# Attention in front of two expert layers: when weights are prepared, when constant rows are filled, and which engine adds the columns of the last batch

## The chip, the cores and the metric

The kernel runs on one core of a Trainium2 chip. The metric is device time in microseconds (us); lower is better. The kernel before was timed at 1121.05 us (median of 3 runs, 1119.55 to 1121.26). The execution that left the profile took 1118.75 us, and the profile's span, from its first to its last instruction, is 1117.0 us.

## The reference, cut to what matters

Three parts are chained. The first is causal attention with a bias made of a running sum of `s`; the second is a sum over 8 experts with a balanced gate; the third is one wide layer with a softplus. The change touches the first part and its seam with the second.

```python
# q, k, v: (2, 8, 576, 64)   s: (2, 8, 576)
cum = np.cumsum(np.maximum(s, 0.0), axis=-1)
bias = -(cum[:, :, :, None] - cum[:, :, None, :])
scores = np.where(causal, -1e9, q @ k.T / 8 + np.minimum(bias, 0.0))
attn = softmax(scores); out = attn @ v
# x = out as (1152, 512): 576 tokens of batch 0, then 576 of batch 1
P = exp(x @ w_gate), rows and columns normalised 8 times in turn
out = sum over e of P[:, e] * (relu(x @ w1[e]) @ w2[e])
out = softplus(out @ w_in) @ w_out
```

## The kernel before, in words

**Attention.** Heads are worked in 8 pairs p = 0 to 7 (pairs 0 to 3 are batch 0, pairs 4 to 7 batch 1), and each pair has 5 units i = 0 to 4: four blocks of 128 query rows, and one block that holds the last 64 rows of both heads. So there are 40 units, numbered n = 0 to 39; unit 6 is (p, i) = (1, 1).

A unit passes through these stages. TensorE computes the scores, adding the running sum by one more product of `bq` and `bk` (L551, L555). VectorE adds the mask and takes the row extreme (L586 to L598). ScalarE takes the exponential (L608), VectorE the reciprocal of its sum (L619), GpSimd multiplies (`eb`, L621). TensorE transposes `eb` (`tr`, L633 to L648), ScalarE copies that to `pt` (L653), and TensorE multiplies by v (`pv`, L665, L675). ScalarE copies the result to `xr` (L724).

The loop at L763 issues, for every n, one step of each stage for a different unit (`LN, LT, LV, LA, LX, LY = 2, 3, 4, 5, 1, 1`), in the order of the letters "YSKAXVWBTED". Every engine runs its instructions strictly in the order issued, so whatever an early instruction waits for holds up all that stand behind it on that engine.

**What is interleaved with it.** Letter K splits the next pair's q and k into a high and a low part (ScalarE L511 `kh`/`qh`, GpSimd L512 `kl`/`ql`). Letter W takes one step of `early_w`, which prepares `w1` of the first expert. Its 32 steps are: two GpSimd sums for each half (L155, L157), splits of ScalarE (L146 `w1h`) and VectorE (L149 `w1l`) with two steps between them, four more GpSimd sums (L162, L164), and six more splits. Letter Y takes up to two steps of `build`, which turns a finished quarter of `xr` into the operands `xh` and `xl` of the expert layer: it forms four differences of column blocks in `xt` (L82), copies high parts on ScalarE (L85) and forms low parts on VectorE (L88). A batch has two builds, c = 0 and c = 1. Only the very last one (batch 1, c = 1, `quick`) has three of its four differences on VectorE; the others have all four on GpSimd, spread over several n.

**Before the loop.** The bias operands `bq`, `bk`, `be` exist twice, set 0 and set 1. Each is cleared and then gets rows of ones or minus ones (`init_bias`, L439): set 1 on VectorE, set 0 on GpSimd. VectorE then takes the running sum (L471, L473), and `cs` holds its two parts (L478, L479). From `cs` come the rows that SP loads into `bk` and `bq` (L452) and `be` (L457). SP issues all loads in program order: after the bias rows of pairs 0 and 1 come q and k of pair 2 (L421), the four raw weight tiles of the first expert (L135, `raw`), v of pair 1 (L428), and the last columns of pair 1's q (L524, `end1h`, `end1l`).

**After it.** The first products of the expert layer (L287) use batch 0 and need ScalarE to copy a partial result (`v`, L295), which stands behind the last build on ScalarE.

Of the kernel before, what the change touches and what calls it, by code (L numbers as in the profile page):

```python
# [20 lines left out]
def attention_moe_ffn(ctx, tc, q, k, v, s, w_gate, w1, w2, w_in, w_out, out):  # L21
    nc = tc.nc
    P = 128
    B, S, H, D = v.shape
# [28 lines left out]
    def f(ap):  # L53
        return ap.bitcast(F32)
# [14 lines left out]
    def build(g, c, xr, xt_pool, quick):  # L69

        h, l = xh[g], xl[g]
        x1, x2 = xr[:, c, :], xr[:, c + 2, :]
        z = x2.rearrange("p (j n) -> p j n", j=2)
        xt = xt_pool.tile([P, 4, HB], F32, tag="xt", name="xt", bufs=1)
        high = [(h[:, B11, c, :], x1[:, :HB]), (h[:, B21:B22 + 1, c, :], z), (h[:, T1:T4 + 1, c, :], xt)]
        low = [l[:, B11, c, :], l[:, B21:B22 + 1, c, :], l[:, T1:T4 + 1, c, :]]
        sums = [(0, x1[:, HB:], x1[:, :HB]), (1, x2[:, HB:], xt[:, 0, :]), (3, x2[:, :HB], xt[:, 1, :]),
                (2, x2[:, HB:], x1[:, HB:])]

        def sum_(n, engine):  # L80
            o, a, b = sums[n]
            engine.tensor_tensor(out=xt[:, o, :], in0=a, in1=b, op=ALU.subtract)  # L82

        def high_(n):
            nc.scalar.activation(out=high[n][0], in_=high[n][1], func=AF.Copy)  # L85

        def low_(n):
            nc.vector.tensor_tensor(out=low[n], in0=high[n][1], in1=f(high[n][0]), op=ALU.subtract)  # L88

        if quick:  # L90
            sum_(3, nc.gpsimd)
            for n in range(3):
                sum_(n, nc.vector)
            for n in range(3):
                high_(n)
            for n in range(3):
                low_(n)
            yield
            return
        high_(0)  # L100
        low_(0)
        yield
        sum_(0, nc.gpsimd)
        yield
        high_(1)
        sum_(3, nc.gpsimd)
        sum_(1, nc.gpsimd)
        yield
        low_(1)
        sum_(2, nc.gpsimd)  # L110
        for _ in range(3):
            yield
        high_(2)
        yield
        low_(2)
        yield
# [281 lines left out]
    with tc.manual_schedule():  # L398
# [3 lines left out]
        with ExitStack() as att:  # L402
# [36 lines left out]
            def init_bias(x, engine):  # L439
                for t in (bq_t[x], bk_t[x], be_t[x]):  # L440
                    engine.memset(f(t), 0.0)
                for j in range(2):
                    for t, cols, one in ((bq_t[x], slice(0, S), 1.0), (bk_t[x], slice(0, S), -1.0),
                                         (be_t[x], slice(j * REM, (j + 1) * REM), 1.0)):
                        engine.memset(f(t[j * D:j * D + 4, cols]), one)

            def load_bias(p):
                for j in range(2):
                    h = 2 * p + j
                    x = c8d[h] if p > 1 else f(cs[h:h + 1])  # L450
                    for t, r, cols in ((bk_t, 2, slice(0, S)), (bq_t, 0, slice(0, S))):
                        (nc.sync if p > 0 or j == 0 else nc.scalar).dma_start(  # L452
                            out=f(t[p % BB][j * D + r:j * D + r + 2, :]), in_=x)
                for j in range(2):
                    h = 2 * p + j
                    x = c8d[h, :, NB * P:] if p > 1 else f(cs[h:h + 1, :, NB * P:])
                    nc.sync.dma_start(out=f(be_t[p % BB][j * D:j * D + 2, j * REM:(j + 1) * REM]), in_=x)  # L457
# [10 lines left out]
            c8 = eb_tile(B * H, "c8")  # L468
            nc.vector.memset(ones, 1.0)
            init_bias(1, nc.vector)  # L470
            nc.vector.tensor_scalar(s_sb, s_sb, 0.0, 8.0, ALU.max, ALU.mult)  # L471
            for a, b, first in ((0, 2 * P, 0.0), (2 * P, S, c8[:, 2 * P - 1:2 * P])):
                nc.vector.tensor_tensor_scan(c8[:, a:b], one_row[:, a:b], s_sb[:, a:b], first, ALU.mult, ALU.add)  # L473
            init_bias(0, nc.gpsimd)
            cs = ac.tile([B * H, 2, S], F32R, name="cs")
            c8d = dr.tile([B * H, 2, S], F32, name="c8d")
            for a, b in ((0, 2 * P), (2 * P, S)):
                nc.scalar.activation(out=cs[:, 0, a:b], in_=c8[:, a:b], func=AF.Copy)  # L478
                nc.vector.tensor_tensor(out=cs[:, 1, a:b], in0=c8[:, a:b], in1=f(cs[:, 0, a:b]), op=ALU.subtract)  # L479
            load_bias(0)  # L480
            make_identity(nc, ident)

            W = NB * P
# [238 lines left out]
            def do_X(n):  # L722
                for pv, o, p in xs.get(n - LX, ()):
                    nc.scalar.activation(out=o, in_=pv, func=AF.Copy)  # L724
                    if p is not None and p % NP >= NP // 2:
                        g, c = p // NP, p % NP - NP // 2
                        building.append(build(g, c, xr, ap2, g + 1 == B and c == 1))
# [28 lines left out]
                        split_ends(p + 1)  # L756

            def do_W(n):
                if n >= 3:
                    next(prework, None)  # L760

            do = dict(S=do_S, T=do_T, V=do_V, A=do_A, X=do_X, Y=do_Y, B=do_B, E=do_E, K=do_K, D=do_D, W=do_W)
            for n in range(nu + LA + LX + 1):  # L763
                now[0] = n
# [228 lines left out]
        x = -1  # L993
# [92 lines left out]
```

## Time and profile before

| what | value |
|---|---|
| median of 3 runs | 1121.05 us |
| profiled execution | 1118.75 us |
| span of its profile | 1117.0 us |
| TensorE (PE) busy | 1080.4 us, 97% |
| VectorE (DVE) busy | 737.8 us, 66% |
| ScalarE (ACT) busy | 528.1 us, 47% |
| GpSimd (POOL) busy | 419.6 us, 38% |

A busy share here is an average over the whole span. The attention takes about the first 121 us, and the expert products follow almost without a gap. Times in rows are counted from the span's start. A row of the timeline is start, duration, engine, line, operation, output and inputs, shape, count, and in brackets the idle time of the engine before it with what ended that idle time. SPq is the queue of the engine that issues loads.

### The profile page before, as it was taken

Reading aid. Unit: us, or ns where it says so; the run is one execution under the profiler, and the core shown is the slowest. Engines: PE = TensorE matmul, PEld = TensorE weight load, DVE = VectorE, ACT = ScalarE, POOL = GpSimd, SP = SyncE. Lnnn points to the kernel's source line nnn. Section 1 sums busy time; section 2 is a strip of 40 time slices with the busy share of each in tenths; the row PEclk is TensorE's granted clock in tenths of the full one; section 3 lists DMA queues with packets and bytes.
Section 4 is the critical chain, followed back from the end, with each engine's and each line's share of the span. In section 5 each row is a group of like instructions: output and inputs, shape, how many; then the busy total and the mean of one; then the engine's idle time right before and its main releaser. Section 6 shows DMA issues by size and latency. Waiting matters only on the chain.

```text
span 1117.0 us, 18144 instructions
## 1 busy us (share of the span) xinstructions
PE 1080.4 (97%) x6692; PEld 951.8 (85%) x6692; DVE 737.8 (66%) x1641; ACT 528.1 (47%) x1246; POOL 419.6 (38%) x493
## 2 busy tenths in 40 slices
PE   4989999999999999999999999999999999999998
PEld 3767789898988988889888898889889898888887
DVE  4456645847878778787878888775555575465553
ACT  3988644233443434334343443334334267656551
POOL 5876411134423324142341523413020065555552
PEclk9999999999999999999999999999999999999999
DMA  5222102032122322223132222311112111111001
GB/s 171 85 78 66 40 1 76 3 112 94 67 94 95 125 83 87 95 94 121 60 114 95 95 90 75 129 58 38 38 39 76 38 39 38 39 38 38 1 11 75
DMA packets 30424, 78.48 MB, mean 70 GB/s; under 512 B 6048, under 2 KB 10656, under 8 KB 30336
## 3 DMA queue, kind: packets, MB, share of 16 engines
q1 hardware_dynamic: 27768, 68.93, 19.1%
q0 software_dynamic: 2560, 8.39, 1.9%
q8 instruction: 52, 0.85, 0.3%
q14 instruction: 36, 0.29, 0.1%
q10 hardware_dynamic: 8, 0.01, 0.0%
HBM read 66.00 MB, written 10.82 MB: 69 GB/s over the span
## 4 chain that ended last, share of the span: by engine, by line
PE 82%; DVE 7%; ACT 5%; POOL 3%; issue 2%; SPq 1%; DMA 0%; POOLq 0%; DVEq 0%; ACTq 0%
PE py L376 41%; PE ph L287 31%; PE ph L351 4%; POOL a L259 2%; PE sc L551 1%; POOL a L258 1%; PE pv L665 1%; DVE a L256 1%; DVE hl L265 1%; PE tr L639 1%; ACT hh L262 1%; ACT a L251 1%; ACT eb L608 1%; PE tr L633 1%; ACT a L250 1%
## 5 line engine op out<-in xcount | busy, mean ns | idle before, releaser
L376 PE MATMUL py<-w2h,hh 128*128 128x512 f32 x720 | 287.2, 399 | 7.4 <-DVE acc L388 6.1
L376 PE MATMUL py<-w2h,hl 128*128 128x512 f32 x720 | 285.2, 396 | 1.0 <-DVE hl L238 1.0
L376 PE MATMUL py<-w2l,hh 128*128 128x512 f32 x720 | 285.2, 396 | 0.0
L287 PE MATMUL ph<-xh,w1h 128*128 128x288 f32 x896 | 265.1, 296 | 2.5 <-ACT v L295 2.5
L287 PE MATMUL ph<-xh,w1l 128*128 128x288 f32 x896 | 264.8, 296 | 0.0
L287 PE MATMUL ph<-xl,w1h 128*128 128x288 f32 x896 | 263.3, 294 | 0.0
L287 PEld LDWEIGHTS ph<-xh,w1h 128*128 128x128 f32 x896 | 167.9, 187 | 20.0 <-ACT v L295 2.8
L287 PEld LDWEIGHTS ph<-xl,w1h 128*128 128x128 f32 x896 | 168.3, 188 | 16.5
L287 PEld LDWEIGHTS ph<-xh,w1l 128*128 128x128 f32 x896 | 168.2, 188 | 0.0
L376 PEld LDWEIGHTS py<-w2h,hl 128*128 128x128 f32 x720 | 135.7, 188 | 34.1 <-DVE hl L238 1.6
L201 POOL TENSOR_TENSOR w2l<-raw,w2h 128x512 fp32r<-128x512 f32 x40 | 55.4, 1384 | 287.4 <-ACT w2h L199 287.4
L235 ACT ACTIVATE hh<-ph 128x288 fp32r<-128x288 f32 x192 | 78.8, 412 | 159.8 <-DVE ph L337 81.2
L376 PEld LDWEIGHTS py<-w2h,hh 128*128 128x128 f32 x720 | 135.5, 188 | 21.2 <-DVE acc L388 6.8
L376 PEld LDWEIGHTS py<-w2l,hh 128*128 128x128 f32 x720 | 135.9, 189 | 11.6
L295 ACT ACTIVATE v<-ph 128x288 f32<-128x288 f32 x128 | 51.0, 411 | 171.7 <-PE ph L287 164.8
L391 DVE SCALAR_TENSOR_TENSOR acc<-py,gate,acc 128x512 f32<-128x512 f32 x126 | 94.0, 746 | 54.2 <-PE py L376 54.0
L894 POOL TENSOR_TENSOR cm<-cm,ct 128x512 f32<-128x512 f32 x32 | 45.1, 1409 | 202.5 <-DVE ct L892 202.5
L238 DVE SCALAR_TENSOR_TENSOR hl<-ph,hh 128x288 fp32r<-128x288 f32 x192 | 86.7, 454 | 30.5 <-ACT hh L235 28.7
L149 DVE TENSOR_TENSOR w1l<-raw,w1h 128x512 fp32r<-128x512 f32 (+1 forms) x144 | 99.8, 694 | 8.3 <-ACT w1h L146 8.2
L265 DVE TENSOR_TENSOR hl<-a,hh 128x288 fp32r<-128x288 f32 x64 | 38.0, 594 | 71.9 <-ACT hh L262 71.9
L146 ACT ACTIVATE w1h<-raw 128x512 fp32r<-128x512 f32 (+1 forms) x144 | 82.9, 577 | 1.6 <-PE ph L287 1.6
L258 POOL TENSOR_TENSOR a<-a,a 128x288 f32<-128x288 f32 x64 | 51.8, 809 | 78.8 <-DVE a L256 61.4
(182 smaller groups left out, 1766.1 us busy)
## 6 DMA issues: line engine op xcount, KB each, us to landing
raw<-in_w SPq DMA_DIRECT2D x64, 512.0 KB
f<-in_w_in SPq DMA_DIRECT2D x16, 512.0 KB
f<-in_w_out SPq DMA_DIRECT2D x16, 512.0 KB
wd<-cm POOLq DMA_DIRECT2D x32, 256.0 KB, 3.2
raw<-wd SPq DMA_DIRECT2D x16, 512.0 KB
out<-acc SPq DMA_DIRECT2D x9, 256.0 KB
vv<-in_v SPq DMA_DIRECT2D x8, 256.0 KB
qk<-in_k SPq DMA_DIRECT2D x7, 288.0 KB
```

Of the source, the lines that this page charges most:

```text
L146: nc.scalar.activation(out=hi[:, o], in_=t[:, src], func=AF.Copy)
L149: nc.vector.tensor_tensor(out=lo[:, o], in0=t[:, src], in1=f(hi[:, o]), op=ALU.subtract)
L201: (nc.gpsimd if i else nc.vector).tensor_tensor(out=lo, in0=t[:, r], in1=f(hi), op=ALU.subtract)
L235: nc.scalar.activation(out=hh, in_=z, func=AF.Relu)
L238: nc.vector.scalar_tensor_tensor(out=hl, in0=z, scalar=0.0, in1=f(hh), op0=ALU.max, op1=ALU.subtract)
L258: nc.gpsimd.tensor_tensor(out=a2, in0=a1, in1=a2, op=ALU.subtract)
L265: nc.vector.tensor_tensor(out=hl, in0=a3, in1=f(hh), op=ALU.subtract)
L287: nc.tensor.matmul(o, u, v, start=(start and c == 0 and n == 0), stop=(c == 1 and n == 2), skip_group_check=True)
L295: nc.scalar.activation(out=t, in_=self.a, func=AF.Copy)
L376: nc.tensor.matmul(py[t], u, v, start=(k == 0 and n == 0), stop=(k == NF - 1 and n == 2))
L391: nc.vector.scalar_tensor_tensor(out=a, in0=py, scalar=gate_t[0][:, t, e:e + 1], in1=a, op0=ALU.mult, op1=ALU.add)
L894: nc.gpsimd.tensor_tensor(out=m, in0=m, in1=f(t), op=ALU.add)
```

## The change

Three edits.

1. `init_bias` is cut in two. It now only clears; a new `init_ones` fills the rows of ones. For set 0 both follow each other on GpSimd as before. For set 1 the clearing stays ahead of the running sum on VectorE, and its six fills move behind the running sum and the first loads of bias rows.
2. `do_W` starts at n = 9 where it started at n = 3, so each step of the first expert's weights comes six units later. The 32 steps fit still: the last comes at n = 41.
3. `build` takes the path with three differences on VectorE for both builds of the last batch. For c = 0 it yields between the parts, so that they spread over n = 41 to 43.

```diff
@@ build
-        if quick:
+        if g + 1 == B:
+
             sum_(3, nc.gpsimd)
             for n in range(3):
                 sum_(n, nc.vector)
             for n in range(3):
                 high_(n)
+                if not quick:
+                    yield
             for n in range(3):
                 low_(n)
+                if not quick:
+                    yield
             yield
             return
@@ init_bias
             def init_bias(x, engine):
                 for t in (bq_t[x], bk_t[x], be_t[x]):
                     engine.memset(f(t), 0.0)
+
+            def init_ones(x, engine):
                 for j in range(2):
                     for t, cols, one in ((bq_t[x], slice(0, S), 1.0), (bk_t[x], slice(0, S), -1.0),
                                          (be_t[x], slice(j * REM, (j + 1) * REM), 1.0)):
@@ before the loop
             init_bias(0, nc.gpsimd)
+            init_ones(0, nc.gpsimd)
...
             load_bias(0)
+            init_ones(1, nc.vector)
             make_identity(nc, ident)
@@ the loop
             def do_W(n):
-                if n >= 3:
+                if n >= 9:
                     next(prework, None)
```

Lines of the changed kernel are 5 to 9 higher than the same lines before.

VectorE in the opening, before: the last three fills of set 1 (`bq_92`, `bk_94`, `be_96`) stand ahead of the running sum `c_112` and its parts `cs`.

```order
L445 MEMSET bq_92 4x576
L445 MEMSET bk_94 4x576
L445 MEMSET be_96 4x64
L471 TENSOR_SCALAR s_sb<-s_sb 16x576
L473 SCALAR_TENSOR_TENSOR c_112<-one_row,s_sb 16x256
L473 SCALAR_TENSOR_TENSOR c_112<-one_row,c_112,s_sb 16x320
L479 TENSOR_TENSOR cs<-c_112,cs 16x256
L479 TENSOR_TENSOR cs<-c_112,cs 16x320
```

VectorE in the opening, now: the running sum follows the last clearing directly.

```order
L446 MEMSET be_96 128x128
L478 TENSOR_SCALAR s_sb<-s_sb 16x576
L480 SCALAR_TENSOR_TENSOR c_112<-one_row,s_sb 16x256
L480 SCALAR_TENSOR_TENSOR c_112<-one_row,c_112,s_sb 16x320
L487 TENSOR_TENSOR cs<-c_112,cs 16x256
L487 TENSOR_TENSOR cs<-c_112,cs 16x320
L452 MEMSET bq_92 4x576
L452 MEMSET bk_94 4x576
L452 MEMSET be_96 4x64
```

All six fills moved from ahead of `s_sb` to behind `cs`.

GpSimd in the first units, before: the sums of the raw weights (`raw_187`, `raw_189`) stand between the scalings of `eb`, whose `st_201` to `st_204` are those of units 0 to 3.

```order
L512 TENSOR_TENSOR ql<-qk,qh 128x576
L621 TENSOR_SCALAR eb<-eb,st_201 128x128 x2
L155 TENSOR_TENSOR raw_187<-raw_187 128x256
L621 TENSOR_SCALAR eb<-eb,st_202 128x256 x2
L157 TENSOR_TENSOR raw_187<-raw_187 128x256
L621 TENSOR_SCALAR eb<-eb,st_203 128x384 x2
L155 TENSOR_TENSOR raw_189<-raw_189 128x256
L621 TENSOR_SCALAR eb<-eb,st_204 128x512 x2
```

GpSimd in the first units, now: nothing of the weights until unit 7.

```order
L521 TENSOR_TENSOR ql<-qk,qh 128x576
L630 TENSOR_SCALAR eb<-eb,st_201 128x128 x2
L630 TENSOR_SCALAR eb<-eb,st_202 128x256 x2
L630 TENSOR_SCALAR eb<-eb,st_203 128x384 x2
L630 TENSOR_SCALAR eb<-eb,st_204 128x512 x2
L521 TENSOR_TENSOR kl<-qk,kh 128x576
L630 TENSOR_SCALAR eb<-eb,st_205 128x576
L521 TENSOR_TENSOR ql<-qk,qh 128x576
L630 TENSOR_SCALAR eb<-eb,st_206 128x128 x2
L630 TENSOR_SCALAR eb<-eb,st_201 128x256 x2
L160 TENSOR_TENSOR raw_187<-raw_187 128x256
```

The first sum of `raw_187` moved from behind unit 0's scaling to behind unit 6's.

VectorE at the end of the attention, before: the two builds of batch 1 (`xl_77`), of which only the second has differences (`xt`) here; `st_204` is unit 39's.

```order
L88 TENSOR_TENSOR xl_77<-xr,xh_75 128x288
L617 TENSOR_REDUCE st_204<-st_204 128x1
L619 RECIPROCAL st_204<-st_204 128x1
L88 TENSOR_TENSOR xl_77<-xr,xh_75 128x2x288
L88 TENSOR_TENSOR xl_77<-xt,xh_75 128x4x288
L82 TENSOR_TENSOR xt<-xr 128x288
L82 TENSOR_TENSOR xt<-xr,xt 128x288 x2
```

VectorE at the end of the attention, now.

```order
L82 TENSOR_TENSOR xt<-xr 128x288
L82 TENSOR_TENSOR xt<-xr,xt 128x288 x2
L626 TENSOR_REDUCE st_204<-st_204 128x1
L628 RECIPROCAL st_204<-st_204 128x1
L88 TENSOR_TENSOR xl_77<-xr,xh_75 128x288
L88 TENSOR_TENSOR xl_77<-xr,xh_75 128x2x288
L88 TENSOR_TENSOR xl_77<-xt,xh_75 128x4x288
```

Three differences of the first build came onto VectorE ahead of unit 39's reciprocal, and its low parts went behind it; the second build is as it was.

## Rows read from the trace of the kernel before

**Rows 1.** Windows, one pair each (three in the second): length, busy PE PEld DVE ACT POOL, clock.

```profile
47.69:59.07 11.38, 11.38 (x124) 8.85 (x125) 6.09 (x34) 10.87 (x32) 9.94 (x15) 1.00 0.30 87
59.07:101.27 42.20, 37.44 (x370) 28.05 (x371) 25.21 (x106) 36.36 (x101) 31.90 (x42) 0.96 0.24 69
101.27:112.66 11.39, 11.39 (x124) 8.85 (x125) 5.84 (x33) 9.69 (x30) 4.75 (x9) 1.00 0.25 80
```

**Rows 2.** Timeline of the opening, 0 to 12 us.

```profile
0.75 0.40 SPq L460 DMA_DIRECT2D s_sb<-in_s  x1
...
1.66 0.43 SPq L421 DMA_DIRECT2D eb<-in_q  x1
...
3.02 0.54 DVE L445 MEMSET bq<- 4x576 f32 x1
...
5.17 0.80 PE L551 MATMUL sc<-eb 64*128 64x128 f32 x4 [5.17 <-DMA eb<-in_q]
...
5.65 0.45 DVE L471 TENSOR_SCALAR s_sb<-s_sb 16x576 f32<-16x576 f32 x1
...
8.34 0.48 DVE L479 TENSOR_TENSOR cs<-c,cs 16x320 fp32r<-16x320 f32 x1 [0.22 <-ACT cs L478]
...
9.69 0.58 SPq L452 DMA_DIRECT2D bq<-cs  x1
...
11.54 0.80 PE L551 MATMUL sc<-bk,bq 64*128 64x128 f32 x2 [5.57 <-DMA bq<-cs]
```

**Rows 3.** Timeline of units 3 and 4, 23 to 25 us.

```profile
23.01 0.72 POOL L155 TENSOR_TENSOR raw<-raw 128x256 f32<-128x256 f32 x1 [5.32 <-DMA raw<-in_w]
23.29 2.04 SPq L524 DMA_DIRECT2D end1l<-ql  x2
...
24.25 1.15 PE L633 MATMUL tr<-ident,eb 128*128 128x128 f32 x4 [5.48 <-POOL eb L621]
```

**Rows 4.** Windows of 1 us: length, PE busy, granted clock, DMA share, GB/s.

```profile
23.00:24.00 1.00, 0.00 (x0) 0.50 0.99 352
...
77.00:78.00 1.00, 1.00 (x11) 0.64 0.09 20
```

**Rows 5.** Chain of waits that ended last: start, length, what.

```profile
18.01 4.93 DMA raw<-in_w
...
34.21 1.06 PE sc L555 x8
...
36.30 0.37 PE tr L633 x2
...
49.42 0.59 PE tr L633 x4
```

**Rows 6.** DMA issues of the page: count and KB of each.

```profile
raw<-in_w SPq DMA_DIRECT2D x64, 512.0 KB
...
qk<-in_k SPq DMA_DIRECT2D x7, 288.0 KB
```

**Rows 7.** Timeline of units 20 to 24, 61 to 76 us.

```profile
61.98 0.62 ACT L146 ACTIVATE w1h<-raw 128x512 fp32r<-128x512 f32 x1
...
64.35 1.41 POOL L512 TENSOR_TENSOR kl<-qk,kh 128x576 fp32r<-128x576 f32 x1 [1.58 <-ACT kh L511]
...
67.80 1.28 DVE L149 TENSOR_TENSOR w1l<-raw,w1h 128x512 fp32r<-128x512 f32 x1
...
69.67 0.42 PE L555 MATMUL sc<-kh,end0h 128*128 128x320 f32 x1 [1.15 <-DVE st L586]
...
71.11 1.63 POOL L621 TENSOR_SCALAR eb<-eb,st 128x128 f32<-128x128 f32 x4
...
75.27 0.63 PE L633 MATMUL tr<-ident,eb 128*128 128x128 f32 x4 [1.52 <-ACT pt L653]
```

**Rows 8.** Line L82 on VectorE from 60 to 126 us: duration least/median/most in ns.

```profile
L82 DVE TENSOR_TENSOR xt<-xr,xt x2: 457/668/878, 123.6 to 124.6; 128x288 f32<-128x288 f32 x2
```

**Rows 9.** Timeline of the first expert products, 126 us.

```profile
126.62 0.40 PE L287 MATMUL ph<-xh,w1h 128*128 128x288 f32 x1 [2.52 <-ACT v L295]
```

## The prediction, made blind

> **What bounds the kernel now.** I read the busy shares first: TensorE is busy 97% of the span, so a change to the attention can only pay where TensorE stands still there, or runs slowly. Windows cut at the first transposes of a pair show where that is. A pair without trouble takes 11.38 us with TensorE busy throughout, and so does the last full one, 11.39 [rows 1]. Three pairs in a row, 4 to 6 less their edges, take 42.20 us in place of 3 x 11.38 = 34.14: 8.1 us are lost there. The timeline of the opening shows TensorE waiting 5.57 us for the first bias row `bq` [rows 2]. The timeline of the units behind it shows one long stop: TensorE waits 5.48 us for GpSimd's scaling of unit 1, and GpSimd itself sat 5.32 us in front of it, at the first sum of the raw weights, for their load [rows 3]. The clock by windows is 0.50 (the 1.2 GHz level) when TensorE comes back [rows 4]. The chain of waits agrees on the place: it runs through that load for 4.93 us [rows 5]. Last, TensorE waits 2.52 us on the seam to the expert layer, for a copy `v` on ScalarE [rows 9]. Behind that point the expert products run almost without a gap, and the change leaves them as they are. So I expect what is saved before the seam to stay saved.
>
> **Term 1, the fills.** Before, VectorE starts the first fill at 3.02 and the running sum at 5.65 [rows 2]. Six fills go from there, 2.63 us. The sum, `cs`, the bias loads and every load that SP issues behind them start earlier by that much, if `s_sb` has arrived at 3.02. The trace shows no wait for it, since VectorE came late. It is issued at 0.75. The short load `bq` was issued at 9.69 and used at 11.54, 1.85 us later; the 288 KB load `eb<-in_q` was issued at 1.66 and used at 5.17, 3.51 us later [rows 2, 6]. So `s_sb` arrives between 2.60 and 4.26, and the term is 2.63 down to 2.63 - (4.26 - 3.02) = 1.39. It is 36 KB, far nearer to the short load; I take 2.6.
>
> The Trainium skill, "DMA: Bandwidth & Descriptors", section "Anatomy of one DMA — SWDGE (gpsimd) path", puts the fixed part of one transfer at about 2.0 us. An estimate by it has `s_sb` there at about 2.8, no wait; the 1.85 us of the trace agrees.
>
> The fills cost the same 2.63 us where they go. VectorE's part of `cs` ends at 8.82, now 6.19, so they end at 8.82 again. What covers them is the bias row's load: its product starts at 11.54 - 2.63 = 8.91 and takes 0.80 [rows 2], and VectorE's first masking waits for that. If the cover failed the price would be what sticks out, under 0.3 us. SP's loads into set 1 come behind pair 0's loads and must wait for the fills too: those before them on SP run past 8.82.
>
> **Term 2, the stop.** With the sums gone from units 3 to 6, GpSimd goes from unit 0's scaling straight to unit 1's. That was held 5.32 us; TensorE had finished its earlier work at 24.25 - 5.48 = 18.77 and had nothing else. I take 5.48, with 5.32 below [rows 3]. The sums come at unit 9, by then about 27 us, when the tiles loaded from 18.01 on have long landed; nobody waits for them before the splits of unit 13, and the first product with these weights comes after the attention.
>
> **Term 3, the clock.** From unit 1's transposes to the next pair's first, TensorE took 36.30 - 24.25 = 12.05 us; over the same work a pair of windows later it took 59.07 - 49.42 = 9.65 [rows 1, 3, 5]. The difference of 2.40 is the stretch at the 0.50 clock, which began while TensorE stood still [rows 4]. Without the stop I count it as saved; the other end is 0, if the clock falls all the same.
>
> **Term 4, what is late next.** The last columns `end1l` are issued up to 25.33 and used at unit 9's scores at 34.21 [rows 3, 5]. Terms 1 to 3 together bring these scores to 34.21 - 10.5 = 23.7, but the loads only to 25.33 - 2.63 = 22.70. With the short load's time behind its issue, 11.54 - 10.27 = 1.27, they arrive at 23.97: a wait of 0.3. The load of `eb<-in_q` needed 5.17 - 2.09 = 3.08 behind its issue: 25.78, a wait of 2.1. And the way is busy: two tiles of 288 KB and four of 512 KB are ahead, 2.69 MB, at 352 GB/s 7.6 us [rows 4, 6]. Counted from 18.01 - 2.63 = 15.4 that is 23.0, with 1.27 more 24.3, a wait of 0.6. I take -0.6, bounds 0 and -2.1. Opening: 2.6 + 5.5 + 2.4 - 0.6 = 9.9 us.
>
> **Term 5, the lossy pairs.** The splits move by six units, and three things change among units 19 to 24. (a) ScalarE's `w1h` of 0.62 leaves unit 20, where ScalarE is full. (b) VectorE's `w1l` of 1.28 leaves unit 22, where TensorE waits 1.15 us for the masking right behind it. (c) GpSimd gets the four second sums in units 19 to 22, where `build` has its differences. Two of them, 2 x 0.72 [rows 3], come between `kl` at 64.35 and the scalings at 71.11 [rows 7], a stretch in which GpSimd never rests. So GpSimd reaches those scalings at 71.11 - 0.62 (an earlier `kh`) + 1.44 = 71.9, while TensorE would be ready for them 0.62 + 1.15 earlier than before: it waits for GpSimd in place of VectorE and gains next to nothing at this point. But ScalarE and VectorE then run ahead, and the next wait, 1.52 us for a copy to `pt` behind the large `xh` [rows 7], shrinks. I take +1.2 of that 1.52. If with fewer gaps the clock does not fall at 77 [rows 4], more than 1 us is added. Bounds: +4.0 (half of the 8.1 us) and -1.5 (the sums, all in TensorE's way).
>
> The splits that come to units 35 to 38 add at most 2 x 0.62 us to ScalarE's 9.69 in a pair of 11.39 [rows 1, 7]: 10.93, hidden. Without that cover, -1.2.
>
> **Term 6, the seam.** Before, the four differences of build c = 0 run on GpSimd behind unit 39's scaling; the large `xh`, the evacuation of the last `xr` and the last build queue up behind them on ScalarE, and at its end the copy `v`. With three on VectorE, the large `xh` has its input some us earlier, and the last build starts when TensorE delivers. VectorE pays by its own row, 0.46 each, 0.88 where GpSimd's difference runs beside it [rows 8]: 3 x 0.46 = 1.4 to 1.8 us, ahead of unit 39's reciprocal, in a place where it took a low part of `build` before. The gain ends where TensorE's wait does, 2.52 [rows 9]. Since the large `xh` also goes ahead of unit 38's copies to `pt`, I take half a us off: +2.0, bounds 0 (ScalarE as late as before) and 2.5.
>
> Against this edit speaks the Trainium skill, "SBUF — State Buffer", section "Who interferes with whom": a VectorE instruction with two inputs in SBUF contends with a GpSimd instruction that reads SBUF. By it one of the three differences runs at the slow figure, as 878 against 457 ns shows [rows 8]. Term 6 would be 2.0 with it and about 2.4 without.
>
> **Sum.** 9.9 + 1.2 + 2.0 = 13.1 us. The profiled execution of 1118.75 us becomes 1105.7, its span of 1117.0 becomes 1103.9. That execution lies 2.3 us under the median of the runs; I subtract from the median: 1121.05 - 13.1 = 1108.0.
>
> **Rivals.**
> - *The opening gives less.* `s_sb` is late (-1.2), `end1l` is late (a further -1.5), and the clock falls in the opening anyway (-2.4). For it: the transfers are near saturation at 352 GB/s, and nothing in the trace shows when `s_sb` lands. Against it: the opening's gap gets shorter, not longer. 13.1 - 5.1 = 8.0: 1113.0 us.
> - *The lossy pairs come free too.* Term 5 at its upper end: 13.1 + 2.8 = 15.9, 1105.2 us. For it: the fall of the clock there follows two waits of which one goes. Against it: the second build, units 26 to 31, has its splits as before.
> - *The change doesn't do what it says.* GpSimd's wait for the raw load goes, but TensorE then waits in the same place for another load of the saturated stretch, and the seam stays. Only the fills' 2.6 us and about as much lost again in term 5: 1121 us.
> - *Slower: the weights become the bound.* Their last split ends six units later, and the next expert's two raw tiles, whose buffers it frees, load later by six units, about 14 us (6 x 11.38 / 5). If that expert's preparation waited for them, ScalarE and VectorE would queue behind it and TensorE with them. It decides from the point where the tiles come over 13.1 us after they are wanted; with 5 us more, 1126. Against it: a tile takes 4.93 us [rows 5] and is wanted only in the first expert's products, behind 126.62.
>
> **Chances.** The forecast, 1106 to 1111 us by itself, 0.60; the weak opening 0.22; free pairs 0.12; no effect 0.03; slower 0.03. The range from 1103.5 to 1113.5 takes in the first three with most of their bounds. A measurement of this kernel tells about 0.2%, 2.2 us, from no change. Faster by more than that 0.94, same 0.03, slower 0.03.
>
> **What would show it.** In the profile after: the running sum at about 3.0 and the first `bq` product at 8.9 (term 1); no wait of GpSimd for `raw` and no TensorE stop over 1 us before 25 us (term 2); clock 1.00 through 20 to 30 us (term 3); unit 9's scores with a wait under 1 us for `end1l` (term 4); the three pairs in about 41 us, with GpSimd as what TensorE waits for near unit 23 (term 5); TensorE's wait for `v` under 1 us (term 6). A new stop of several us ahead of the `end` columns, or a seam still waiting 2.5 us, would make the prediction wrong.

## The result, and the profile after

The changed kernel takes 1107.55 us (median of 4 runs, 1107.13 to 1108.51) against 1120.86 us before (1119.55 to 1121.26, 4 runs): a ratio of 0.9884, 95% interval 0.9867 to 0.9902, or 11.0 to 14.9 us. The forecast was 1108.0. The profiled execution took 1107.13 us with a span of 1105.4.

One profile of each kernel is one execution, so both kernels were profiled twice more (e9 to e12 below). The table puts the three profiled executions of each side by side: starts in the timeline, in us (the windows of [rows 1] are cut 0.07 later).

| point | before | after | change of the means |
|---|---|---|---|
| first transposes of unit 1 | 24.25, 25.56, 25.97 | 17.38, 17.08, 16.23 | -8.4 |
| first transposes of pair 1 | 36.23, 37.59, 37.65 | 29.80, 29.83, 30.63 | -7.1 |
| first transposes of pair 3 | 59.00, 60.36, 60.43 | 52.58, 53.55, 53.40 | -6.8 |
| first transposes of pair 6 | 101.20, 102.56, 102.59 | 93.60, 96.01, 96.83 | -6.6 |
| first gate product `pg`, behind the seam | 131.82, 133.16, 133.18 | 122.25, 124.65, 125.48 | -8.6 |
| end of the span | 1117.0, 1118.2, 1118.2 | 1105.4, 1107.9, 1110.2 | -10.0 |

So the attention gives 8.6 us, and the 13.3 between the medians hold more than the terms of the prediction name. The three pairs differ: up to `pg` the first one gives 9.6 us and the other two 8.1 on the mean, up to the end of the span 11.6 and about 9. These are rows of the timeline of after, first profile.

```profile
2.88 0.43 DVE L478 TENSOR_SCALAR s_sb<-s_sb 16x576 f32<-16x576 f32 x1
...
8.65 0.44 PE L560 MATMUL sc<-bk,bq 64*128 64x128 f32 x1 [2.87 <-DMA bq<-cs]
...
11.57 1.09 PE L560 MATMUL sc<-bk,bq 64*128 64x384 f32 x1
...
13.38 1.41 PE L560 MATMUL sc<-bk,bq 64*128 64x512 f32 x1
...
16.58 0.38 PE L642 MATMUL tr<-ident,eb 128*128 128x128 f32 x2
...
17.38 0.66 PE L642 MATMUL tr<-ident,eb 128*128 128x128 f32 x4
...
20.00 1.29 SPq L533 DMA_DIRECT2D end1h<-qh  x2
...
27.49 0.38 PE L564 MATMUL sc<-kh,end1h 128*128 128x320 f32 x1 [2.14 <-DMA end1h<-qh]
...
65.60 0.68 PE L642 MATMUL tr<-ident,eb 128*128 128x128 f32 x2 [1.56 <-POOL eb L630]
...
106.27 0.57 DVE L82 TENSOR_TENSOR xt<-xr 128x288 f32<-128x288 f32 x1
107.29 1.32 DVE L82 TENSOR_TENSOR xt<-xr,xt 128x288 f32<-128x288 f32 x2 [0.45 <-ACT xr L733]
...
116.61 0.39 ACT L300 ACTIVATE v<-ph 128x288 f32<-128x288 f32 x1
...
117.06 0.40 PE L292 MATMUL ph<-xh,w1h 128*128 128x288 f32 x1
```

The running sum starts at 2.88 and the first `bq` product at 8.65, where [rows 2] has 5.65 and 11.54. The 5.48 us stop of [rows 3] is gone: unit 1's transposes follow unit 0's within 0.8 us. A new stop stands at 27.49, 2.14 us for `end1h`. Near unit 20 TensorE now waits for GpSimd, where [rows 7] has VectorE and ScalarE. At the seam `v` is ready when it is wanted; the 2.52 us of [rows 9] are gone. The chain of waits of the same kernel (start, length, what) shows what the new stop hangs on:

```profile
20.65 6.70 DMA end1h<-qh
```

And the windows (length; busy PE PEld DVE ACT POOL; clock, DMA share, GB/s) show a pair without trouble, the lossy three one by one, and their sum:

```profile
29.87:41.27 11.40, 11.40 (x125) 8.86 (x125) 5.59 (x33) 10.35 (x30) 9.70 (x15) 1.00 0.29 88
...
52.65:65.60 12.95, 11.39 (x123) 8.77 (x124) 5.88 (x29) 12.20 (x35) 11.89 (x16) 1.00 0.26 77
65.60:80.01 14.41, 13.16 (x124) 10.00 (x124) 10.16 (x36) 11.91 (x33) 12.36 (x16) 0.88 0.24 69
80.01:93.67 13.66, 12.37 (x124) 9.15 (x125) 8.79 (x40) 12.02 (x34) 9.71 (x15) 1.00 0.11 29
52.65:93.67 41.02, 36.92 (x370) 27.92 (x371) 24.84 (x105) 36.13 (x100) 33.96 (x45) 0.96 0.20 58
```

The three pairs take 41.02 where [rows 1] has 42.20. In the middle one the clock mean of 0.88 shows a fall that came behind the stop of 1.56.

### The profile page after: what moved, and what is told of

The parts are those of the page before. It is cut to its first block, busy times and chain, and to the rows that moved or that the text cites. A ratio compares the mean times of both kernels' runs of the same rounds, so it can differ in the third digit from the quotient of the medians.

```text
span 1105.4 us, 18149 instructions
## 1 busy us (share of the span) xinstructions
PE 1077.6 (97%) x6692; PEld 949.1 (86%) x6692; DVE 739.5 (67%) x1644; ACT 526.1 (48%) x1246; POOL 417.8 (38%) x490
## 4 chain that ended last, share of the span: by engine, by line
PE 82%; DVE 6%; ACT 4%; POOL 4%; issue 2%; DMA 1%; POOLq 0%; SPq 0%; ACTq 0%; DVEq 0%
PE py L381 41%; PE ph L292 32%; PE ph L356 4%; POOL a L264 2%; PE sc L560 2%; DVE hl L270 1%; PE pv L674 1%; POOL a L263 1%; DVE a L261 1%; PE tr L648 1%; ACT hh L267 1%; ACT eb L617 1%; DMA end1h<-qh 1%; PE sc L564 1%; ACT a L256 1%
## 5 line engine op out<-in xcount | busy, mean ns | idle before, releaser
L381 PEld LDWEIGHTS py<-w2l,hh 128*128 128x128 f32 x720 | 135.5, 188 | 11.6
```

The lines of the kernel that those rows point to most:

```text
L381: nc.tensor.matmul(py[t], u, v, start=(k == 0 and n == 0), stop=(k == NF - 1 and n == 2))
```

## The experiments

Differences of times are against the 1120.56 us (16 runs) or 1120.73 us (8 runs) that the kernel before took on the same chip.

**e1: the weights' steps alone, on the kernel before.**

```diff
-                if n >= 3:
+                if n >= 9:
```

> The kernel before with the weights' steps from unit 9 alone. Theory A (the opening is set by when the end columns land, and that time hangs on SP's queue, which this edit alone does not move): TensorE no longer waits for GpSimd, but waits about 3.6 us for end1h at unit 9's scores, which start at about 30.0 in place of 34.2; with 1.2 us from the lossy pairs the kernel gains about 5.3 us, 1115.6. Rival B (the terms add up as in the prediction): the stop, the clock and the lossy pairs give 5.5 + 2.4 - 0.6 + 1.2 = 8.5 us, 1112.4, with a wait under 1 us for end1h.

Measured 1115.46 us (ratio 0.996, 0.9946 to 0.9973): 5.1 less, the amount that theory A says. Its timeline:

```profile
29.42 0.38 PE L555 MATMUL sc<-kh,end1h 128*128 128x320 f32 x1 [1.06 <-DMA end1h<-qh]
...
121.29 0.61 PE L287 MATMUL ph<-xh,w1h 128*128 128x288 f32 x1 [2.48 <-ACT v L295]
```

The wait for `end1h` takes the place of the stop, though it is 1.06 and not the 3.6 expected; the seam still waits. So this edit alone brings the raw load's stop down to a wait for the next load in line.

**e2: the fills alone, on the kernel before.**

```diff
+            def init_ones(x, engine):
...
+            init_ones(0, nc.gpsimd)
...
+            init_ones(1, nc.vector)
```

> The kernel before with the six fills behind the running sum alone. Theory A: every load comes 2.6 us earlier, so the raw weights land earlier and GpSimd's wait for them ends earlier by as much: 2.6 us gained, 1118.3, with unit 1's transposes at 21.6 in place of 24.25. Rival B (what counts is when TensorE gets through pair 0, which in the changed kernel came only 1.3 us earlier, since its products there run at half the speed of later ones): 1.3 us, 1119.6.

Measured 1116.97 us (0.9969, 0.9959 to 0.9979): 3.6 less, a microsecond more than the 2.6 of theory A. Its timeline:

```profile
21.24 0.89 PE L637 MATMUL tr<-ident,eb 128*128 128x128 f32 x4 [3.88 <-POOL eb L625]
```

The stop for the raw weights is 3.88 where the kernel before has 5.48, 5.75 and 6.27. In that one profile the load is used 4.73 us behind its issue (15.28 to 20.01); in the three executions of the kernel before that takes 5.00, 6.32 and 6.59. With such a spread in one kernel it is not shown that the earlier issue made the load faster, and where the extra microsecond comes from stays open.

**e3: the column sums of the last batch alone, on the kernel before.**

```diff
-        if quick:
+        if g + 1 == B:
```

> The kernel before with batch 1's first build on VectorE alone. Theory A: the seam gives its 2.0 us by itself, 1118.9, TensorE's wait for v falls from 2.5 us to under 0.6, and the first expert product starts about 0.6 us later. Rival B: the last build is late whatever the first does, no gain, 1120.9.

Measured 1116.9 us (0.997, 0.996 to 0.9981): 3.7 less. In its profile the wait for `v` is gone, and from pair 6's transposes to `pg` it takes 132.00 - 103.61 = 28.39 us; before takes 30.62, 30.60 and 30.59. The seam gives 2.2, then, as A says. The other 1.5 us of the timed difference are not at the seam; its one profile does not show where they are.

**e4: the two raw tiles of `w2` loaded later, on the kernel after.** They stand ahead of `end1h` on SP and are wanted only in the expert layer. Here they go to unit 9.

```diff
-            for which in (1, 2):
-                for i in range(2):
-                    load(0, which, i)
+            for i in range(2):
+                load(0, 1, i)
...
+                if n == 9:
+                    for i in range(2):
+                        load(0, 2, i)
```

> The changed kernel with the two raw w2 tiles of the first expert loaded behind unit 9's step in place of before the loop; all else as it is. Theory A: the 1 MB that goes from ahead of the end columns brings end1h about 3 us earlier, TensorE's wait of 2.14 us for it goes, and the kernel gains 2.1 us: 1105.4. Rival B (end1h is late because SP issues it late, not because of what is ahead in the queues): the wait stays at 2.1 us, 1107.5. Rival C: the two tiles now hold up bias rows or v of a later pair on SP, and a new wait eats the gain: 1107.5 or more.

Measured 1107.02 us (0.9892, 0.9876 to 0.9907), no different from after. No wait for `end1h`: pair 1 starts at 26.37, 3.4 earlier than after. But the tiles now stand ahead of the next bias rows. Its timeline and its chain:

```profile
39.20 0.67 PE L560 MATMUL sc<-bk,bq 64*128 64x128 f32 x2 [0.57 <-DMA bq<-c8d]
```

```profile
35.23 3.83 DMA bq<-c8d
```

The next pair takes 12.57 us instead of 11.4, and a part of the gain is given back there. Two things qualify the 3.4. Unit 1's transposes come at 16.25 against 17.38, so 1.1 of it is there before `end1h` matters: here the products of 512 columns in pair 0 ran at full speed, which varies between executions (e10). And SP itself comes to `end1h` earlier:

```profile
16.25 0.43 SPq L433 DMA_DIRECT2D vv<-in_v  x1
16.72 0.56 SPq L434 DMA_DIRECT2D vv<-in_v  x1
17.39 1.78 SPq L533 DMA_DIRECT2D end1h<-qh  x2
```

In after the row of `end1h` stands at 20.00. SP issues two tiles fewer, and the two loads of v behind the tiles take 0.43 and 0.56 us to issue where they took 1.12 and 1.55. So the wait comes of the two tiles, but rival B is not ruled out as a part of it: how much they cost at SP's issue and how much in the queues is not separated.

**e5: the same two tiles at unit 34**, behind the last bias rows.

```diff
+                if n == 34:
+                    for i in range(2):
+                        load(0, 2, i)
```

> The changed kernel with the two raw w2 tiles loaded behind unit 34, where the loads of attention are through. In e4 (behind unit 9) the wait for end1h went, pair 1's first transposes came at 26.44 in place of 29.87, but the next pair waited for a bias row behind the two tiles and 1.2 us went again. Theory A (both waits are the price of what is ahead in the queues): neither wait is left, all of the 3.4 us of pair 1 reach the first expert product, at 110.3 in place of 113.6, and the kernel gains 3.4 us on the changed one: 1104.1. Rival B (the wait for the bias row comes of SP's order, not of the tiles): as in e4, 2.1 us, 1105.4.

Measured 1105.72 us (0.9866, 0.985 to 0.9882). Neither wait is left, and the clock stays at 1.00 up to pair 4. Pair 3's first transposes come at 49.12, 3.5 to 4.4 us ahead of the three executions of after; the first expert product comes at 110.23, as A had it (110.3). The median fell by 1.8 only, near the number of B, though the wait that B names is not there. The profile shows the rest behind the seam: here the clock falls behind the second long stop of the wide layer (1020 to 1023 us), which it does not in the first profile of after. A row of pair 0, for e6, and for the lossy pairs a row of its timeline and its window:

```profile
11.58 1.09 PE L560 MATMUL sc<-bk,bq 64*128 64x384 f32 x1
...
62.17 0.68 PE L641 MATMUL tr<-ident,eb 128*128 128x128 f32 x2 [1.58 <-POOL eb L629]
```

```profile
49.12:90.20 41.08, 38.25 (x371) 29.10 (x369) 24.83 (x104) 36.30 (x101) 34.03 (x45) 0.92 0.20 58
```

**e6: e5, and TensorE kept busy before the first bias row.** 17 products of ones by ones, whose results nobody reads, around the first scores.

```diff
+            def warm_up(k):
+                for _ in range(k):
+                    nc.tensor.matmul(warm[:, :P], ones, ones, start=True, stop=True)
+
+            warm_up(9)
```

> e5 with 9 products of ones by ones on TensorE ahead of the first scores and 8 between them and the first bias product, where TensorE only waits; their result is not used. Theory A (pair 0's products take twice as long as later ones because TensorE was idle before them and its clock is at the lower level, though the clock column reads 1.00 there): the 512-column bias products of pair 0 fall from about 0.8 to 1.4 us to about 0.4, unit 0's transposes come at 15.0 to 15.5 in place of 16.58, and 1.1 to 1.6 us are gained on e5: 1102.8. Rival B (they are long because of operands in float32 and of waits for masking): durations as before, no gain, 1104.1. Rival C: the products stand in the way and the first bias product is later than 8.65.

Measured 1106.02 us (0.9868, 0.9854 to 0.9882): nothing over e5. Its timeline:

```profile
10.63 0.63 PE L560 MATMUL sc<-bk,bq 64*128 64x384 f32 x1
...
14.84 0.68 PE L650 MATMUL tr<-ident,eb 128*128 128x128 f32 x2 [0.74 <-POOL eb L638]
...
24.04 0.38 PE L566 MATMUL sc<-kh,end1h 128*128 128x320 f32 x1 [0.46 <-DMA end1h<-qh]
```

The bias product of 384 columns takes 0.63 us, where e5 and after have 1.09: A's durations hold, pair 0's products run at full speed from 8.7 us on. (The products of 512 columns tell nothing here: e5 too has 0.80 for them.) What they win is taken by GpSimd's scaling (0.74) and `end1h` (0.46): pair 1 starts at 26.38, in e5 at 26.35.

**e7: after without the four second sums of the first expert.**

```diff
-            if x < NX:
+            if 0 < x < NX:
...
+            if x == 0:
+                for _ in range(4):
+                    yield
```

> The changed kernel without the four second sums of the first expert's raw weights on GpSimd (units 19 to 22); the output of that expert is then not the reference's. Theory A (term 5: GpSimd has become what TensorE waits for near unit 23): the wait of 1.56 us at unit 20's transposes goes or falls under 0.4, and the three pairs from 52.65 take 0.5 to 1.2 us less than 41.02. Rival B (the next wait, for the copy to pt and for masking, takes it): the wait goes but the three pairs take 41.0 as before.

One execution, 1112.32 us, with 4.36 us of waiting for `end1h` in its opening, so only the lossy pairs are read. Timeline and window:

```profile
68.14 0.68 PE L645 MATMUL tr<-ident,eb 128*128 128x128 f32 x2 [0.27 <-POOL eb L633]
71.19 0.63 PE L645 MATMUL tr<-ident,eb 128*128 128x128 f32 x4 [1.02 <-ACT pt L665]
```

```profile
56.42:98.61 42.19, 37.49 (x371) 28.15 (x370) 24.55 (x104) 36.83 (x102) 32.01 (x42) 0.96 0.19 57
```

GpSimd's wait of 1.56 shrinks to 0.27: the second sums did make it. But ScalarE's copy is late next, by 1.02, and the three pairs take 42.19, inside the 41.02 to 43.43 of after. In this one execution taking the sums away gains nothing, as B has it.

**e8: e5, with one step of `build` for each unit instead of two, up to unit 39.**

```diff
-                for _ in range(2):
+                for _ in range(1 if n < 40 else 2):
```

> e5 with one step of build per unit in place of two before unit 40, so that batch 0's two builds spread over units 21 to 36. Theory A (the three lossy pairs lose about 7 us because the pieces of a build come together and stand ahead of masking and of the copies to pt): the loss falls by 2 to 4 us, to about 1101. Rival B (the loss is the sum of the work on ScalarE and VectorE, wherever it stands, or mostly the one large piece of xh and xl): no gain, 1104.1, or a loss where the second build now meets the splits of units 32 to 35.

Measured 1104.06 us (1103.63 to 1104.57; 0.985, 0.9837 to 0.9864), the fastest of all. Timeline and window:

```profile
64.42 0.89 PE L641 MATMUL tr<-ident,eb 128*128 128x128 f32 x4 [0.81 <-POOL eb L629]
```

```profile
50.16:88.24 38.08, 35.60 (x371) 26.85 (x369) 24.56 (x105) 34.93 (x100) 32.94 (x42) 1.00 0.21 63
```

The wait of 1.58 becomes 0.81, the clock stays at 1.00, and the three pairs lose 38.08 - 34.14 = 3.9 us in place of 6.9. Most of these 3.0 us are not waits: TensorE stands still for 38.08 - 35.60 = 2.5 us here and for 41.08 - 38.25 = 2.8 in e5, while its busy time is 2.65 us less, because in e5 the clock falls (0.92) and here it does not. That the shorter wait kept it up is likely and not shown, since falls vary between executions of one kernel (below). The opening of this profile was a microsecond later than that of e5; `pg` comes 1.7 us earlier, and the medians, of 5 and 4 runs, are 1.7 apart too.

**e9 and e10: the kernel after as it is, twice more. e11 and e12: the kernel before, twice more.** Another chip, one execution each.

> The changed kernel as it is, looked at once more. In the profiles so far the wide layer at the end shows one of two pictures behind the same stop of about 2.0 us (TensorE waits for VectorE's acc): the granted clock falls to 0.50 for some 3 to 4 us (before, and the single edits e1, e2, e3, and e5, e8), or it stays 1.00 (after, e4, e6, e7). From the product behind the copy v (pg) to the end that is about 985.0 us with the fall and 983.2 without. Theory A: whether it falls varies between executions of one kernel and is no effect of the change; then about half of the looks at after show it, and the time from pg to the end is 985 in those. Theory B: the kernel decides it (its place in time at the start shifts everything behind); then this look shows none again, 983.2 us, and both looks at before show it.

> The same kernel, a third look. A: a fall in one of the two looks, or in both; B: none in either, clock 1.00 from 1015 to 1040 us, 983.2 us from pg to the end. In either case the first products of pair 0 run at their half-speed durations again (1.41 us for 512 columns), and the wait for end1h is between 1 and 4 us, by how fast the raw tiles land.

> The kernel before as it is, looked at once more. A: the clock stays at 1.00 behind the wide layer's stop in one of the two looks at before, and pg to the end is then about 983.2 us. B: it falls in both, 985 us. The stop for the raw load near 24 us is between 4.9 and 6.2 us (5.48 in the first look, 6.10 in e3, whose opening is that of before).

> The same, a third look at before: A no fall in one of the two, B a fall in both. The differences of the two kernels over the attention alone (first product of the opening to pg) should be 9.6 us in any of these looks, give or take the 1 us by which the raw load's landing varies.

Measured 1109.78 and 1111.95 us for after, 1119.97 and 1119.94 for before. The wide layer has three long stops. Behind the second, which the expectations mean, there is a fall in e10 and none in e9, a fall in e11 and none in e12. Theory A holds: one kernel does both. (The 1.41 us that e10's text expects again for 512 columns were 0.80; its 384 columns still took the half-speed 1.09.) The windows of e10, then those of e12, and one of the first profile of after, behind its third stop:

```profile
26.00:28.00 2.00, 1.14 (x4) 1.18 (x5) 0.00 (x0) 0.33 (x2) 0.00 (x0) 0.70 0.55 164
28.00:30.00 2.00, 2.00 (x15) 1.78 (x16) 0.74 (x4) 0.00 (x0) 0.03 (x1) 0.50 0.04 12
...
53.40:96.83 43.43, 40.98 (x371) 31.22 (x370) 24.72 (x104) 36.87 (x102) 33.96 (x45) 0.84 0.18 55
...
1025.00:1030.00 5.00, 3.69 (x13) 3.21 (x13) 4.43 (x10) 3.23 (x9) 3.07 (x4) 0.69 0.01 3
```

```profile
982.00:988.00 6.00, 6.00 (x28) 5.41 (x27) 3.81 (x8) 2.83 (x7) 3.25 (x4) 0.72 0.00 1
...
1035.00:1040.00 5.00, 4.11 (x24) 3.72 (x25) 4.22 (x8) 3.04 (x7) 3.49 (x4) 1.00 0.01 3
```

```profile
1076.00:1082.00 6.00, 6.00 (x27) 5.44 (x28) 2.59 (x7) 2.19 (x5) 3.18 (x5) 0.72 0.23 87
```

The wide layer stops TensorE three times for VectorE's `acc`, by some 5.6 to 6.1 us in all, in every execution. Behind the third stop the clock falls in all six. Behind the first two there is one fall in each execution of before (in e12 behind the first), and none, none and one after. From `pg` to the end that makes 985.2, 985.0 and 985.0 us before, and 983.2, 983.3 and 984.7 after. The two of after with and without show that such a fall costs about 1.5 us. Another 0.3 is the first stop itself, 1.94 to 1.97 us before and 1.63 to 1.66 after; what shortened it stays open.

Not expected: in e9 and e10 the clock falls in the opening as well. The timelines of e9 and e10, in that order:

```profile
26.96 0.38 PE L564 MATMUL sc<-kh,end1h 128*128 128x320 f32 x1 [1.91 <-DMA end1h<-qh]
```

```profile
26.86 0.61 PE L564 MATMUL sc<-kh,end1h 128*128 128x320 f32 x1 [2.67 <-DMA end1h<-qh]
```

and the windows of e9:

```profile
28.00:30.00 2.00, 2.00 (x20) 1.53 (x20) 1.33 (x7) 0.07 (x1) 0.81 (x2) 0.67 0.03 7
30.00:32.00 2.00, 2.00 (x22) 1.55 (x24) 0.51 (x6) 1.67 (x4) 1.03 (x2) 0.50 0.03 8
...
53.55:96.01 42.46, 37.56 (x372) 28.00 (x370) 24.77 (x104) 36.79 (x102) 34.03 (x45) 0.96 0.19 56
```

A stop of 2.14 us was followed by full speed, one of 1.91 by the 1.2 GHz level. So the length of a stop alone does not tell whether the clock falls. The rise at the start varies as well: the first products of 512 columns took 1.41 us in the first profile of after and in e9, 0.80 in e10. Of this rise the Trainium skill says in "TensorE: Matmul & The Clock Gate", section "What's actually happening", that its point depends on where the first product falls in a window which runs freely; these executions agree. For the falls no run shows more than that they vary.

## Why the prediction was right, and where it was not

The sign and the parts of the kernel were right, and so was the time, in part by luck, as the end of this section shows. By its own terms, with two rows of the timeline of after, first profile, and one of its windows, for term 4:

```profile
17.18 1.12 SPq L433 DMA_DIRECT2D vv<-in_v  x1
18.34 1.55 SPq L434 DMA_DIRECT2D vv<-in_v  x1
```

```profile
15.00:27.00 12.00, 10.22 (x85) 7.31 (x85) 6.95 (x37) 10.64 (x31) 9.67 (x16) 1.00 0.87 281
```

- **Term 1, the fills: right.** Forecast 2.6. `s_sb` is not waited for, the first `bq` product comes 2.9 us earlier each time, and unit 0's transposes 2.5 us on the mean (17.90, 18.95, 18.84 to 16.58, 16.29, 15.43). In the first pair it is only 1.3, since there the late products of pair 0 ran slower after (1.41 us for 512 columns) than before (0.89). The fills' new place cost nothing that shows. The 2.0 us that the prediction takes from the Trainium skill, "DMA: Bandwidth & Descriptors", section "Anatomy of one DMA — SWDGE (gpsimd) path", stand there for loads issued by GpSimd. `s_sb` is issued by SP; that it had landed is shown by the row at 2.88, which has no wait.
- **Term 2, the stop: right.** Terms 1 and 2 together said 8.1 at unit 1's transposes; the table has 8.4 on the mean, from 6.9 in the first pair to 9.7.
- **Term 4, `end1h`: the step that failed.** The loads' arrival was put at 24.3, at the latest 25.78, and the wait at 0.6. TensorE gets to go on at 27.49, 26.96 and 26.86, after waits of 2.14, 1.91 and 2.67, all near or over the upper bound. The step priced the landing behind the big tiles as their volume by the bandwidth plus the 1.27 us of a short load alone, and two sizes in it were off. It left out v of pair 1, two loads of 256 and 32 KB that also stand ahead of `end1h`; and it took 352 GB/s, the rate of one full microsecond, where the stretch from 15 to 27 us moved 281. An estimate with both, (2.69 + 0.29) MB at 281 GB/s from the first tile's issue at 15.28, and 1.27 more, gives 27.2; the chain has 20.65 + 6.70 = 27.35. e4 and e5 show that the two `w2` tiles make the wait: with them out of the way it is gone and pair 1 starts 3.4 us earlier, of which 1.1 is pair 0's clock. The Trainium skill, "DMA: Bandwidth & Descriptors", section "Queues, rings and completion order", has each DMA engine take descriptors in the order of their ring; e4, where the same tiles delay the next bias rows, agrees.
- **Term 3, the clock: half right.** 2.4 us were booked as saved. The fall of [rows 4] went with its stop, but a new one came behind the wait of term 4 in two of three executions. From unit 9's scores to pair 1's transposes e9 and e10 take 2.87 and 3.77 us against 2.31; in e9 the next pair also takes 12.34 instead of 11.39.
- **The opening as a whole: 6.8 to 7.1 us where 9.9 was said.** Of the 2.8 to 3.1 missing, 1.6 are the wait (2.24 on the mean, less 0.6) and about 1.0 the clock behind it (0, 1.5 and 1.5). This is the rival of the weak opening, by the second and third of its three mechanisms, and not the forecast.
- **Term 5, the lossy pairs: the place right, the amount not.** GpSimd is what TensorE waits for near unit 20 each time (1.56, 1.58, 1.56). The 1.2 us came out in the first pair of profiles (42.20 to 41.02) and not in the others: 42.46 and 43.43, against 42.20 and 42.16 before. The mean is 0.1 longer, no gain. e7 says why the amount was never safe: with that wait removed, the next engine is late instead. And the clock weighs as much as the waits: in e10 TensorE stands still for only 43.43 - 40.98 = 2.45 us of the three pairs, the least of the three, and yet they take longest, at a mean clock of 0.84.
- **Term 6, the seam: right.** From pair 6's transposes to `pg` it takes 30.60 us before and 28.65 after in all three, so 1.95 of the 2.0. VectorE paid 0.57 + 1.32 = 1.9 us for the three differences, a little over the 1.8 allowed.

That is 8.6 of 13.1 us. The timed 13.3 came out close to it all the same, for reasons that the terms do not hold, and that is luck. The first pair of profiles gives 9.6 up to `pg`. Another 2.0 us lie behind `pg`, where nothing was changed: about 1.5 are a fall of the clock that only one of the two has, the rest is mostly the shorter first stop. The last 1.7 are that the first profile of before lies 2.1 us below the median of its runs and that of after 0.4. The four timed executions of after lie between 1107.13 and 1108.51, the two later ones at 1109.78 and 1111.95. By the three profiles of each alone the change is worth 10 us, by the two later ones about 9, less than the interval of the timed runs and still inside the range of the prediction. How often each fall comes on each chip three executions cannot say. The single edits gave 5.1, 3.6 and 3.7, together 12.4, between the 13.3 of the medians and the 10 of the profiles; no run shows whether they add up.

## What to carry to other kernels

When a load's stop is removed, the load next in line on the same queue is the new bound: count every load ahead of it, price them at the rate of the whole stretch and not of its best microsecond, and move those that are wanted later (in the medians e5 took 1.8 us more). A stop of TensorE has two prices, its length and a stretch at the 1.2 GHz level behind it that may or may not come; a term below 2 us that rests on the second is not shown by one profile of each kernel. Where engines crowd, spreading a helper's steps (e8) was worth 1.7 us in the medians; moving another helper's steps by six units (term 5) was worth nothing on the mean.

## What was not expected of the hardware

In the opening the window rows give a clock of 1.00 while products run at half speed. This is a window of the first profile of after:

```profile
11.00:12.00 1.00, 1.00 (x9) 0.87 (x5) 0.84 (x5) 0.94 (x3) 0.41 (x1) 1.00 0.05 12
```

The product of 384 columns that starts in it takes 1.09 us, against 0.63 behind a busy TensorE (e6). And the same `raw` load makes GpSimd sit 5.32, 6.02 and 6.29 us in three executions of the same kernel.
